# First microseconds of a fused Mamba-2 and feed-forward kernel: idle products, selectors and the first loads

## The chip, the cores and the metric

The kernel runs on one core of a Trainium2 chip. The metric is device microseconds (us) of the whole program. Before the change three runs gave a median of 351.07 us (350.63 to 353.28).

## The reference

Two blocks follow each other. The first is a Mamba-2 state space block for 4 batches, 8 heads, 768 positions, head dimension 32 and state dimension 16. Its recurrence is computed chunk by chunk:

```python
log_a = np.log(np.clip(a, 1e-06, 1.0))
cum = np.cumsum(la, axis=-1)
L = np.exp(cum[:, :, :, None] - cum[:, :, None, :]) * causal
CB = np.einsum('bhin,bhjn->bhij', Cc, Bc)
y = (CB * L) @ xc  +  (Cc @ state) * np.exp(cum)[:, :, :, None]
state = decay_full * state + sum_j Bc x xc * exp(cum[-1] - cum[j])
```

The second takes its output as 3072 tokens of 256 features through a feed-forward block: `h = x @ w_in` (256 to 2048), `g = h * sigmoid(1.702 h)`, `out = g @ w_out` (2048 to 256). The inputs x, a, B and C are float32. The weights are float64 and reach the kernel as pairs of 32-bit words.

## The kernel before

Tokens are worked in six groups of 512, each two "pairs" of two 128-position chunks. For a group the state space part gives `yT` (features on the partitions), then come hidden products with `w_in`, the activation, and products with `w_out`. From the second group on the products are mixed (a scheme with seven products in place of eight). The weights are turned from float64 words to float32 on VectorE and ScalarE piece by piece (`fetch` loads a piece, then `fields`, `clamp`, `rounded`, `join`), and piece i serves a few hidden products, so the first group's hidden products follow the arrival of the weights.

The order on each engine is the order in which the program text issues its instructions; `in_order` at the end fixes it. Waits between engines follow from the data and from the reuse of buffers.

The change touches only the first group, whose start is done in its own way:

- Four loads bring `a` of the first two batches to `az0`, two from SP and two from ScalarE (L274). `load_first` (L134) then loads C with four transfers that ScalarE issues and B with four that SP issues. SP goes on with the first weight piece (`fetch(0)`, L180) and with x of the first two pairs (L150).
- GpSimd makes constants with memsets and affine selects: `pick0` (L300, L303), `ident`, `below` (L316, L318), `same` (L367 to L371, full tile 128x8x32), `pick` (picker, L300 and L303 once more), `whose` (L376, L379), and the zero column of `drop` (L719). `pick` and `whose` are selectors: columns of zeros and ones that pick heads. `part` (VectorE, L387) is summed from `same`.
- `az0` is clamped on VectorE (L338), ScalarE takes the logarithm (L340), and a scan on VectorE makes `cum` (L342).
- On TensorE `keep_busy(5, 0)` (L437) makes five products of ones with ones into the bank `busy`. Nothing reads them. Then eight products with the identity put the causal mask into eight banks (`mask`, L545); `differ` (L551) adds the differences of `cum`, and ScalarE takes the exponential from there (L572). The pool `ps` has four banks, so the bank of the last mask is the one that `busy` had. `pads(n, t)` makes n products of 32 by 32.
- VectorE transposes C and B in 32-blocks (`turn_first`, L612), GpSimd masks C by head (`mask_first`, L645), TensorE turns B back (L624) and makes the scores (L677) and, with `whose`, the rows of `cum` for all heads (L509). VectorE weighs the decays by the scores (`weigh`, L688). Between the two weighings a memset (L171) writes into the buffer of the next weight piece, and SP's next loads (L180, `fetch(1)`) wait for it.
- GpSimd's `since_start` (L662) follows for two pairs. ScalarE's `pick_a` (L363) reads `pick` only in the first group's seventh hidden step.

Of the kernel before, what the change touches and what calls it, by code (L numbers as in the profile page):

```python
# [8 lines left out]
FP32 = mybir.dt.float32  # L9
# [3 lines left out]
ALU = mybir.AluOpType  # L13
AX = mybir.AxisListType

GELU_SCALE = 1.702
P = 128
# [18 lines left out]
def kernel(  # L36
# [31 lines left out]
    nc = tc.nc  # L68
# [4 lines left out]
    NB, NH, S, D = x.shape  # L73
    N = B.shape[-1]
# [10 lines left out]
    PG = CG // 2  # L85
    R = 4
    Q = NH // R
# [7 lines left out]
    const = ctx.enter_context(tc.tile_pool(name="const", bufs=1))  # L95
    raw = ctx.enter_context(tc.tile_pool(name="raw", bufs=3))
    wide = ctx.enter_context(tc.tile_pool(name="wide", bufs=2))
    ssd = ctx.enter_context(tc.tile_pool(name="ssd", bufs=2))
# [30 lines left out]
    def load_first(name, queues):  # L129

        src = {"B": B, "C": C}[name]
        t = blocks[name, 0] = raw.tile([P, 2, PG * P], FP32, tag="z", name=f"z{name}0", bufs=2)
        for r in range(R):
            queues[r].dma_start(  # L134
                out=t[32 * r:32 * r + 32],
                in_=src[0, Q * r:Q * r + Q, :TG].rearrange("q (i f) n -> i q (f n)", i=32))
# [61 lines left out]
    def clamp(i):  # L198


        e = power[i]
        z = e.bitcast(FP32)
        nc.scalar.activation(z, e, AF.Relu, scale=-8.0, bias=edge[:, 0:1])
        nc.scalar.activation(e, z, AF.Relu, scale=-1.0, bias=edge[:, 1:2])
# [68 lines left out]
    for r in range(R):  # L273
        (nc.sync, nc.scalar)[r % 2].dma_start(  # L274
            out=az0[32 * r:32 * r + 32].rearrange("p k s -> p (k s)"),
            in_=a[:2, :, :TG].rearrange("b h (c s) -> (b h) c s", c=PG))
# [3 lines left out]
    def table(f):  # L280

        nc.scalar.activation(early, early, f)

    table(AF.Ln)
    load_first("C", [nc.scalar] * R)
    load_first("B", [nc.sync] * R)
    fetch(0)
    load(0, "x")
# [9 lines left out]
    def picker(name, n, head, group):  # L298
        t = const.tile([P, n, Q], FP32, name=name)
        nc.gpsimd.memset(t, 1.0)  # L300
        for r in range(R):
            rows = t[32 * r:32 * r + 32]
            nc.gpsimd.affine_select(out=rows, in_=rows, pattern=[[-group, n], [-head, Q]],  # L303
                                    compare_op=ALU.is_equal, fill=0.0, base=-head * Q * r,
                                    channel_multiplier=1)
        return t
# [3 lines left out]
    ident = const.tile([P, P], FP32, name="ident")  # L310
# [6 lines left out]
    for side in SIDES:  # L317
        nc.gpsimd.affine_select(out=below[side], in_=below[side], pattern=[[1, H]],  # L318
                                compare_op=ALU.is_ge, fill=-1e5, base=0,
                                channel_multiplier=-1)  # L320
# [9 lines left out]
    def fold_ident(k, engine=nc.vector):  # L330
# [6 lines left out]
    fold_ident(0)  # L337
    nc.vector.tensor_scalar(out=az0, in0=az0, scalar1=1e-6, scalar2=1.0, op0=ALU.max,  # L338
                            op1=ALU.min)
    nc.scalar.activation(cum, az0, AF.Ln)  # L340
    table(AF.Exp)
    nc.vector.tensor_tensor_scan(  # L342
        out=cum.rearrange("p k s -> p (k s)"), data0=carry.rearrange("p k s -> p (k s)"),
# [13 lines left out]
    def pick_a(p):  # L357
# [5 lines left out]
            nc.scalar.activation(X[:, :, q], az[:, c:c + 2], AF.Copy, scale=pick[:, b, q:q + 1])  # L363


    same = ssd.tile([P, NH, D], FP32, tag="BT", name="same")
    nc.gpsimd.memset(same, 1.0)  # L367
    nc.gpsimd.affine_select(
        out=same, in_=same, pattern=[[-N, NH], [0, D]], compare_op=ALU.is_ge,
        fill=0.0, base=0, channel_multiplier=1)  # L370
    nc.gpsimd.affine_select(  # L371
        out=same, in_=same, pattern=[[N, NH], [0, D]], compare_op=ALU.is_ge,
        fill=0.0, base=N - 1, channel_multiplier=-1)
    pick = picker("pick", NB, 1, NH)
    whose = const.tile([32 * PG, 1 + PG, NH, N], FP32, name="whose")
    nc.gpsimd.memset(whose, 1.0)  # L376
    for i, n, head in ((0, 1, PG), (1, 2, PG), (0, 0, 1)):
        t = whose[32 * i:32 * i + 32, n:n + 1]
        nc.gpsimd.affine_select(out=t, in_=t, pattern=[[-1, 1], [-head, NH], [0, N]],  # L379
                                compare_op=ALU.is_equal, fill=0.0, base=-max(n - 1, 0),  # L380
                                channel_multiplier=1)

    part = const.tile([P, Q], FP32, name="part")
    nc.vector.tensor_reduce(  # L387
        out=part, in_=same[:, :, 0].rearrange("p (r q) -> p q r", q=Q), op=ALU.add, axis=AX.X)


    Ls, BE, st = {}, {}, {}
# [33 lines left out]
    def pads(n, t):  # L425

        for i in range(n):
            c = 32 * (i % R)
            nc.tensor.matmul(out=t[c:c + 32, :32], lhsT=ones[:32, :32], rhs=ones[:32, :32],
                             start=True, stop=True, tile_position=(0, c), skip_group_check=True)  # L430

    def keep_busy(n, m):

        t = busy
        pads(m, t)
        for i in range(n):
            nc.tensor.matmul(out=t[:, :3 * H], lhsT=ones,  # L437
                             rhs=ones[:, :H].unsqueeze(1).to_broadcast([P, 3, H]),
                             start=True, stop=True, skip_group_check=True)
# [138 lines left out]
    def bank(name):  # L578
        return ps.tile([P, 4 * P], FP32, tag="ff", name=name)

    def area(name):
        return psa.tile([P, R, 4 * P], FP32, tag="cb", name=name)
# [73 lines left out]
    def since_start(p, engine=nc.vector):  # L656

        b, c = divmod(2 * p, NC)
        s = st[p]
        tp = s["tp"]  # L660
        s["CsT"] = ssd.tile([P, 2, P], FP32, tag="CsT", name=f"CsT{p}", bufs=3)
        engine.tensor_tensor(out=s["CsT"], in0=tp, in1=since[b][:, c:c + 2], op=ALU.mult)  # L662
# [66 lines left out]
    def keep_first():  # L729

        flat_steps = steps.rearrange("p e m -> p (e m)")
        nc.vector.tensor_tensor_scan(
            out=flat_steps, data0=drop.rearrange("p e m -> p (e m)"), data1=flat_steps,
            initial=0.0, op0=ALU.mult, op1=ALU.add)
        for p, copy in zip(range(PG), (nc.vector.tensor_copy, nc.scalar.copy)):
            state[p] = ssd.tile([P, 4, Q * D], FP32, tag="S", name=f"S{p}", bufs=3)
            copy(state[p], steps.rearrange("p e m -> p m e")[:, 4 * p:4 * p + 4])
# [336 lines left out]
    def combine(g):  # L1074


        u, c = copies(g)
        a = acc[g][1]
        scaled(u[:, 2], a[:, 2], u[:, 0])
        scaled(u[:, 1:3], a[:, 3:5], u[:, 2:3].to_broadcast([P, 2, HT]))  # L1080
        scaled(c[:, 1, 0], a[:, 6], u[:, 2])
        scaled(c[:, 0], a[:, 1:6:4], u[:, 0:2])
        plus(c[:, 1, 1], u[:, 2], u[:, 3])
        sums[g] = c
# [51 lines left out]
    def mask_banks(p, r, t, new=True):  # L1136
        ab[p, r] = t[:, :2 * Q * H]
        mask(ab[p, r], new)
# [4 lines left out]
    busy = bank("busy")  # L1143
# [5 lines left out]
                             rhs=ones[:, :H].unsqueeze(1).to_broadcast([P, 4, H]),  # L1149
                             start=True, stop=True, skip_group_check=True)  # L1150

    keep_busy(5, 0)
    both = area("ab0")
    for r in range(R):
        mask_banks(0, r, both[:, r])
    for r in range(R):
        if r == R - 1:
            pads(0, busy)
        mask_banks(1, r, bank(f"ab1_{r}"))
    turn_first("C")  # L1160
    turn_first("B")
# [21 lines left out]
    parts_first()  # L1183
    for p in range(PG):
        since_start(p, nc.gpsimd)
    clamp(0)
    keep_first()
    dense(2)
# [32 lines left out]
    n, p = 2 * PG, 3 * PG  # L1221
# [106 lines left out]
    for g in range(2, NG):  # L1328
        n, p = (g + 1) * PG, (g + 2) * PG
# [14 lines left out]
        def mask_third(k):  # L1344
            if g == 2:
                mask_blocks(k)

        run(g, "1.1 t 0.S P 0.4 P P 1.6 u P 0.3 b 0.T v P 1.5 P 1.7 1.2 P 1.D C", seven(g - 1, 7),
            C=lambda: combine(g - 1), t=turn_third, b=start_third, u=lambda: mask_third(n),
# [82 lines left out]
```

## Time and profile before

| | before |
|---|---|
| median of 3 runs | 351.07 us (350.63 to 353.28) |
| profiled execution: its time | 352.58 us |
| profiled execution: its span, first to last instruction | 350.7 us |
| TensorE busy | 342.9 us, 98% of the span |
| VectorE busy | 255.7 us, 73% |
| ScalarE busy | 149.9 us, 43% |
| GpSimd busy | 13.1 us, 4% |
| DMA | 25.92 MB, mean 74 GB/s |

In the profile PE is TensorE's matmuls and PEld its weight loads, DVE is VectorE, ACT ScalarE, POOL GpSimd, SP the queue that issues most loads; a q behind a name is the engine's sequencer (waits and DMA issues). L with a number is a line of the kernel. One float32 product shows as two records. Starts are in us from the first instruction of the span.

### The profile page before, as it was taken

Reading aid. Unit: us, or ns where it says so; the run is one execution under the profiler, and the core shown is the slowest. Engines: PE = TensorE matmul, PEld = TensorE weight load, DVE = VectorE, ACT = ScalarE, POOL = GpSimd, SP = SyncE. Lnnn points to the kernel's source line nnn. Section 1 sums busy time; section 2 is a strip of 40 time slices with the busy share of each in tenths; the row PEclk is TensorE's granted clock in tenths of the full one; section 3 lists DMA queues with packets and bytes.
Section 4 is the critical chain, followed back from the end, with each engine's and each line's share of the span. In section 5 each row is a group of like instructions: output and inputs, shape, how many; then the busy total and the mean of one; then the engine's idle time right before and its main releaser. Section 6 shows DMA issues by size and latency. Waiting matters only on the chain.

```text
span 350.7 us, 8109 instructions
## 1 busy us (share of the span) xinstructions
PE 342.9 (98%) x3386; PEld 273.8 (78%) x3386; DVE 255.7 (73%) x481; ACT 149.9 (43%) x334; POOL 13.1 (4%) x41
## 2 busy tenths in 40 slices
PE   8889999998999999999999999999999999999996
PEld 7634444546888888888888888888888888889996
DVE  5979999999778999648997457788464654455463
ACT  4788684005353322644432544432554331553320
POOL 8300000100000100000000000000000000000000
PEclk9999999999999999999999999999999999999999
DMA  6599899563625400436604027400000300000301
GB/s 158 110 340 203 223 216 191 85 95 71 111 41 124 72 0 2 75 60 124 115 21 63 0 53 132 76 0 3 0 4 2 54 9 0 0 2 0 62 0 61
DMA packets 89980, 25.92 MB, mean 74 GB/s; under 512 B 73432, under 2 KB 87128, under 8 KB 89944
## 3 DMA queue, kind: packets, MB, share of 16 engines
q1 hardware_dynamic: 89112, 24.88, 34.6%
q10 hardware_dynamic: 832, 0.52, 0.5%
q8 instruction: 26, 0.43, 0.5%
q14 instruction: 10, 0.08, 0.1%
HBM read 22.15 MB, written 3.24 MB: 72 GB/s over the span
## 4 chain that ended last, share of the span: by engine, by line
PE 94%; DVE 2%; DMA 2%; SPq 1%; issue 0%; ACT 0%; DVEq 0%
PE acc L1037 28%; PE X L932 19%; PE Y L942 14%; PE h L876 9%; PE o L974 8%; PE acc L1044 7%; PE y L820 2%; PE cb L677 2%; DMA bits<-in_moe_w_in_dram 2%; PE y L808 1%; PE A L708 1%; PE busy L437 1%; PE ab L551 1%; SPq L180 1%; PE ab L545 0%
## 5 line engine op out<-in xcount | busy, mean ns | idle before, releaser
L937 ACT ACTIVATE ac<-X 128x256 f32<-128x256 f32 x76 | 29.1, 383 | 78.6 <-PE X L932 78.2
L1037 PE MATMUL acc<-mg,mw 128*128 128x256 f32 x192 | 54.5, 379 | 0.0
L909 ACT ACTIVATE gT<-gT 128x512 f32<-128x512 f32 (+1 forms) x76 | 39.3, 520 | 33.9 <-DVE gT L1064 33.3
L1064 DVE TENSOR_TENSOR gT<-Y,ac 128x512 f32<-128x512 f32 x38 | 26.2, 689 | 36.2 <-PE Y L942 30.4
L932 PE MATMUL X<-my,mi 128*128 128x256 f32 x152 | 45.2, 380 | 0.0
L1064 DVE TENSOR_TENSOR gT<-Y,b 128x256 f32<-128x256 f32 x38 | 15.9, 419 | 34.8 <-PE Y L942 34.8
L1037 PEld LDWEIGHTS acc<-mg,mw 128*128 128x128 f32 x192 | 36.5, 190 | 5.0
L876 PE MATMUL h<-yT,w_in 128*128 128x512 f32 (+2 forms) x108 | 35.9, 487 | 1.5 <-DVE w_in L225 1.5
L1037 PE MATMUL acc<-gT,w_out 128*128 128x256 f32 x128 | 35.5, 379 | 0.0
L876 PEld LDWEIGHTS h<-yT,w_in 128*128 128x128 f32 x108 | 18.2, 190 | 17.7 <-issue 15.2
L932 PEld LDWEIGHTS X<-my,mi 128*128 128x128 f32 x152 | 28.0, 190 | 3.9 <-ACT ac L937 0.3
L974 PE MATMUL o<-gT,w_out 128*128 128x512 f32 x64 | 28.6, 597 | 0.0
L900 DVE TENSOR_TENSOR mg<-gT 128x512 f32<-128x512 f32 x40 | 27.2, 681 | 0.0
L1037 PEld LDWEIGHTS acc<-gT,w_out 128*128 128x128 f32 x128 | 24.2, 190 | 3.4 <-ACT yT L847 0.2
L937 ACT ACTIVATE b<-X 128x256 f32<-128x256 f32 x38 | 14.6, 384 | 20.2 <-PE X L932 19.7
L932 PE MATMUL X<-yT,w_in 128*128 128x256 f32 x76 | 23.2, 389 | 0.0
L942 PE MATMUL Y<-my,mi 128*128 128x256 f32 x76 | 22.7, 381 | 0.1
L942 PE MATMUL Y<-yT,w_in 128*128 128x256 f32 x76 | 22.7, 381 | 0.0
L942 PE MATMUL Y<-yT,mi 128*128 128x256 f32 x76 | 22.5, 379 | 0.0
L932 PE MATMUL X<-my,w_in 128*128 128x256 f32 x76 | 22.5, 379 | 0.0
L974 PEld LDWEIGHTS o<-gT,w_out 128*128 128x128 f32 x64 | 11.8, 190 | 13.2 <-issue 12.8
L399 DVE TENSOR_TENSOR_SCAN L<-a,idents 128x1024 f32<-128x1024 f32 x9 | 20.5, 2278 | 0.3 <-DMA a<-scratch 0.3
(152 smaller groups left out, 544.8 us busy)
## 6 DMA issues: line engine op xcount, KB each, us to landing
a<-scratch SPq DMA_DIRECT2D x18, 256.0 KB, 5.3
bits<-in_moe_w_out_dram SPq DMA_DIRECT2D x8, 512.0 KB, 5.1
x<-in_x_dram SPq DMA_DIRECT2D x24, 128.0 KB, 3.6
out_dram<-ob SPq DMA_DIRECT2D x40, 64.0 KB, 1.9
bits<-in_moe_w_in_dram SPq DMA_DIRECT2D x8, 256.0 KB, 5.0
bits<-in_moe_w_in_dram SPq DMA_DIRECT2D x4, 512.0 KB, 8.0
b<-in_B_dram SPq DMA_DIRECT2D x20, 64.0 KB, 2.9
af<-in_a_dram SPq DMA_DIRECT2D x3, 384.0 KB
```

What stands on the lines that cost most here:

```text
L399: nc.vector.tensor_tensor_scan(out=L, data0=ra[p].rearrange("p k e -> p (k e)"), data1=idents.rearrange("p h i -> p (h i)"), initial=0.0, ...
L677: nc.tensor.matmul(out=s["cb"][side, r, k].rearrange("p (q i) -> p q i", q=Q), lhsT=BT[rows, k, side], rhs=CT[rows, k, :, side], start=Tru ...
L876: nc.tensor.matmul(out=h[:, cols], lhsT=w_in[:, f, k], rhs=yT[g][:, k, cols], start=(k == 0 and e == 0), stop=(k == NK - 1), skip_group_ch ...
L900: nc.vector.tensor_tensor(out=t[:, 0:2], in0=B[:, :, 1], in1=B[:, 0], op=ALU.subtract)
L909: nc.scalar.activation(o, i, AF.Silu, scale=GELU_SCALE)
L932: nc.tensor.matmul(out=s["X"], lhsT=lhsT, rhs=rhs, start=i == "1", stop=i == "4", skip_group_check=True)
L937: nc.scalar.activation(copy, s["X"], AF.Copy)
L942: nc.tensor.matmul(out=o, lhsT=lhsT, rhs=rhs, start=s.pop("new", False), stop=i != "5", skip_group_check=True)
L974: nc.tensor.matmul(out=o[c], lhsT=w_out[:, c, f], rhs=gT[g, f // 2][:, f % 2], start=(f == 0), stop=(f == NF - 1), skip_group_check=True)
L1037: nc.tensor.matmul(out=acc[g][0][i][:, cols], lhsT=w, rhs=h[:, cols], start=(j == 0 and k == 0 and (i, 0) in begins), stop=(j == NF // 2 - ...
L1044: nc.tensor.matmul(out=o[k] if type(o) is list else o[:, cols], lhsT=h[:, cols], rhs=w, start=(j == 0 and (i, k) in begins), stop=(j == NF ...
L1064: nc.vector.tensor_tensor(out=o, in0=v, in1=w, op=ALU.add)
```

## The change

`keep_busy` makes three products instead of five, and two 32-by-32 pads go ahead of the last mask. C is loaded with two transfers from each of the two queues, ahead of B on SP's. `same` shrinks to 128x8. `whose` is no longer built by GpSimd: ScalarE copies its three parts from columns of `ident`, ahead of the logarithm. `pick` is built after `since_start`.

```diff
-    load_first("C", [nc.scalar] * R)
+    load_first("C", [nc.sync, nc.scalar] * PG)
     load_first("B", [nc.sync] * R)
     fetch(0)
...
     fold_ident(0)
     nc.vector.tensor_scalar(out=az0, in0=az0, scalar1=1e-6, scalar2=1.0, op0=ALU.max,
                             op1=ALU.min)
+    whose = const.tile([32 * PG, 1 + PG, NH, N], FP32, name="whose")
+    for i, n, head in ((0, 1, PG), (1, 2, PG), (0, 0, 1)):
+        e = 32 * i + max(n - 1, 0)
+        nc.scalar.copy(whose[32 * i:32 * i + 32, n],
+                       ident[32 * i:32 * i + 32, e:e + head * NH:head].unsqueeze(2).to_broadcast(
+                           [32, NH, N]))
     nc.scalar.activation(cum, az0, AF.Ln)
...
-    same = ssd.tile([P, NH, D], FP32, tag="BT", name="same")
+    same = const.tile([P, NH], FP32, name="same")
     nc.gpsimd.memset(same, 1.0)
     nc.gpsimd.affine_select(
-        out=same, in_=same, pattern=[[-N, NH], [0, D]], compare_op=ALU.is_ge,
+        out=same, in_=same, pattern=[[-N, NH]], compare_op=ALU.is_ge,
         fill=0.0, base=0, channel_multiplier=1)
     nc.gpsimd.affine_select(
-        out=same, in_=same, pattern=[[N, NH], [0, D]], compare_op=ALU.is_ge,
+        out=same, in_=same, pattern=[[N, NH]], compare_op=ALU.is_ge,
         fill=0.0, base=N - 1, channel_multiplier=-1)
-    pick = picker("pick", NB, 1, NH)
-    whose = const.tile([32 * PG, 1 + PG, NH, N], FP32, name="whose")
-    nc.gpsimd.memset(whose, 1.0)
-    for i, n, head in ((0, 1, PG), (1, 2, PG), (0, 0, 1)):
-        t = whose[32 * i:32 * i + 32, n:n + 1]
-        nc.gpsimd.affine_select(out=t, in_=t, pattern=[[-1, 1], [-head, NH], [0, N]],
-                                compare_op=ALU.is_equal, fill=0.0, base=-max(n - 1, 0),
-                                channel_multiplier=1)
     part = const.tile([P, Q], FP32, name="part")
     nc.vector.tensor_reduce(
-        out=part, in_=same[:, :, 0].rearrange("p (r q) -> p q r", q=Q), op=ALU.add, axis=AX.X)
+        out=part, in_=same.rearrange("p (r q) -> p q r", q=Q), op=ALU.add, axis=AX.X)
...
-    keep_busy(5, 0)
+    keep_busy(3, 0)
     both = area("ab0")
     for r in range(R):
         mask_banks(0, r, both[:, r])
     for r in range(R):
         if r == R - 1:
-            pads(0, busy)
+            pads(2, busy)
         mask_banks(1, r, bank(f"ab1_{r}"))
...
     for p in range(PG):
         since_start(p, nc.gpsimd)
+    pick = picker("pick", NB, 1, NH)
     clamp(0)
```

## The prediction

> **What bounds the kernel now.** I read the busy table first (TensorE is busy for 98% of the span, so only stretches in which it waits or does filler can be won), then the chain of waits cut to the first 30 us, because every edited line runs there, then the order in time of each engine. The chain, with start, length and owner:
>
> ```profile
> 1.21 3.57 PE busy L437 x10
> 4.78 1.71 PE ab L545 x8
> 6.48 2.60 PE ab L551 x96
> 9.09 0.37 ACT L L572
> ...
> 12.14 1.25 DVE L L688 x2
> ...
> 13.42 0.37 SPq L180
> ...
> 15.63 5.38 DMA bits<-in_moe_w_in_dram
> ...
> 23.33 6.67 PE h L876 x15
> ```
>
> To be seen: the chain begins with five idle products (`keep_busy`, L437) and eight mask products (L545). The decay products (L551) start only when these are through. Then the line is unbroken through exponential (L572), turn back (L624), scores (L677) and the first weighing (L688) to the release of the second weight load (SP, L180), and through that transfer to hidden products 2 and on at 23.33. TensorE idles 1.51 us just before those, so the path through L688 decides, not the first two hidden products. From 23.33 TensorE runs to 37.46 without an idle entry. So a shift of L551 moves the end by as much, if nothing on the way becomes later than it.
>
> The second input of L551 is `cum`, which isn't in this chain. These are rows of all engines in order of time from 4.1 us on (start, length, engine, line; in brackets the idle time before and who ended it):
>
> ```profile
> 4.21 0.45 POOL L371 TENSOR_SCALAR_AFFINE_SELECT same<-same 128x256 f32<-128x256 f32 x1
> 4.22 0.57 DVE L338 TENSOR_SCALAR az<-az 128x256 f32<-128x256 f32 x1 [0.40 <-DMA az<-in_a_dram]
> ...
> 4.83 0.42 ACT L340 ACTIVATE cum<-az 128x256 f32<-128x256 f32 x1 [1.18 <-DVE az L338]
> ...
> 5.28 0.69 DVE L342 TENSOR_TENSOR_SCAN cum<-carry,cum 128x256 f32<-128x256 f32 x1 [0.48 <-ACT cum L340]
> ...
> 7.93 2.03 POOL L645 TENSOR_TENSOR CT<-Ct,part 128x512 f32<-128x512 f32 x2
> ...
> 8.63 1.62 DVE L192 TENSOR_SCALAR p<-bits 128x512 uint32<-128x512 uint32 x1
> ```
>
> `cum` is complete at 5.28 + 0.69 = 5.97; L551's first record begins at 6.41 in the same view, so today TensorE's own queue is 0.44 late. The clamp L338 began 0.01 us after GpSimd's select L371 and ended 0.15 after it; L192, which takes 0.42 to 0.43 us elsewhere, took 1.62 and ended 0.29 after GpSimd's L645 (9.96). Both look blocked by GpSimd.
>
> [...] its record of the granted clock begins at full speed at 6.52 us[...]; the idle products stream 192 columns in 0.32 us, the later filler L1148 256 in 0.22. [...] Here SP spends 0.33 to 0.61 us on each B load.
>
> **The change part by part.**
> - Idle products, five to three. Two products are four records of 0.32: 1.28 us. Masks would begin at 4.57 - 1.28 = 3.29; their operand `below` is complete on GpSimd at 3.21 and identb at 2.75. They run at half clock as now, 0.213 apart: seven end streaming at 4.78.
> - Two pads ahead of the last mask. They write `busy`, whose bank the last mask reuses, so that mask waits for them. No row shows a 32x32 product here; bounds are nothing and 0.5 us (a 128x192 record is 0.53 end to end); I take 0.35. The last mask streams from 5.15 to 5.36. Queued behind it is only L551, which by then waits for `cum`. Cover gone (if `cum` came before 5.36), the cost would be the whole 0.35.
> - GpSimd shorter. `same` falls from three instructions on 128x256 (0.31 + 0.48 + 0.45) to 128x8, about 0.10 + 0.20 + 0.20 by the rows of pick0 (0.10 and 0.19); it ends near 3.9, `drop` near 4.1. So L338 isn't blocked: 4.22 + 0.29 = 4.51, where 0.29 lies halfway by elements between unblocked L192 (512 elements, 0.43) and L322 (4 elements, 0.16). Bounds: nothing gained, if the 0.57 is its own length, to 0.29; I take 0.29, for the two blocked rows agree.
> - Three ScalarE copies ahead of the logarithm. None is in the trace. [...] They wait for `ident` (2.49) and stand behind the table activation (ends 3.65) and ScalarE's second C issue, which now waits for the first load of `a` (landed 3.04) and ends about 3.5. [...] What waits behind them is the logarithm, due at 4.54. [...]
> - `cum`: clamp to 4.51, logarithm 4.54 to 4.96, scan 4.99 to 5.68. L551 begins at 5.74 instead of 6.41: 0.67 earlier.
> - C first on both queues. SP issues two C loads, then four B, the two halves of the first weights and four x: two more than before, about 0.9 us later for all that follows, B's last issue ending near 5.4 instead of 4.44. C's last issue ends at 3.7 instead of 4.19; it landed 2.2 to 2.7 us after its start, so 5.7 to 5.9 instead of 6.49. SP's third B load now waits for the last load of a (landed 4.10), before its own turn at about 4.4: nothing. B: 6.67 becomes 7.4 to 7.6. VectorE: C's transpose 5.95 to 7.0, B's 7.5 to 8.55; TensorE needs B's at 9.45 - 0.6 = 8.85, so 0.3 us spare. First weights: landed 8.53, now 9.0 to 9.4; L192 then no longer meets GpSimd (its two masks end at about 9.1), and L195, Be, L208 end at 11.3 to 11.5, when L688 can start at 12.14 - 0.6 = 11.5: spare 0 to 0.2. x's last load: 11.75 becomes 12.2 to 12.7, which can hold up the gains, but these feed the state and the first hidden products, with the 1.5 us of idle TensorE behind them. SP itself waits 4.3 us for L171 before the next weights.
> - `pick` later: 0.25 + 1.31 us of GpSimd after the two CsT (about 13 us); its first reader is the fan of pair 2, past 35 us. Free; early, it cost GpSimd time only.
>
> Sum: 0.67, less the clock. In the profiled phase L551 would run from 5.74 to 6.52 at half clock: 0.78 us doing 0.39 of work, against 0.05 lost today, so 0.33 is left. [...] I take 0.45. The profiled execution: 350.7 span + 1.9 around it = 352.58, becoming 352.1. It stands 1.5 above the median of the runs; the saving is the same there: 351.07 - 0.45 = 350.6. I hold 350.0 to 351.0 for this case.
>
> **The rivals.**
> - *The clock [...] later (slower).* TensorE has two gaps now, about 0.35 us at the pads and 0.38 before 5.74[...] the turn back and scores take up to 1.3 more: +1.5 to +3, and in the middle 353.3. [...]
> - *The transfers take the place of the wait.* First weights landing after 9.6 or B after 7.9 puts VectorE's row ahead of the scores: the gain is spent and the time is 351.1. For it: the spare of 0.2 us, and a DMA share of 0.77 to 1.20 in every stretch from 4.2 to 9.4 us. Against: with the engines that full, later issue need not be later landing.
> - *The clamp isn't relieved, or the copies are slow.* Then L551 begins at 6.03: 0.38 less the clock's 0.2, 350.9.
>
> **How the numbers follow.** Forecast 0.60, late clock 0.15, transfers 0.15, clamp or copies 0.10. The forecast alone spans 350.0 to 351.0; the runs of before spread over 2.65 us, so a median of three may be off by 0.7, giving 349.3 below. Upwards, the transfers reach 351.8 with that, and the late clock's lower half must be in: 353.0. One per cent, 3.5 us, is about what a measurement of this kernel can tell from no change. Only the far end of the late clock (354.1, with the noise of a median 354.8) gets there: slower 0.05, faster 0.02, same 0.93.
>
> **What would show it.** Right: L338 at 0.3 us; L340 starting by 4.6; L551 by 5.8; L192 at 0.43; L688 near 11.6; hidden product 2 near 22.8. Late clock: the record of full speed begins after 9 us and the L551 rows of 0.65 us are near 1.1. Transfers: an idle entry of L192 or L612 on DMA, and L688 after 12 with TensorE waiting less than VectorE. The forecast is wrong if L688 doesn't move by 0.3 to 0.7, or if it moves and hidden product 2 doesn't.

## The result, and the profile after

The change takes 353.38 us (median; 351.63 to 358.74), the kernel before in the same session 351.71 us (349.62 to 353.71). The ratio is 1.0059, with a 95% interval of 1.0041 to 1.0076: slower by 2.1 us by the ratio and 1.7 by the medians, where 0.45 us less was forecast. Ratios, here and below, leave out executions that took over 1.5% longer than the fastest of their kernel, and the medians keep them. The 351.07 us that the forecast started from is a median of three.

The puzzle is in the profile, which shows nothing of this. Its execution took 351.93 us, near the low end of the change's range, with a span of 350.0 us, and its first microseconds went nearly as the prediction said, step by step. Rows of all engines in order of time (start, length, engine, line, operation; in brackets the idle time before and who ended it):

```profile
3.29 1.70 PE L539 MATMUL ab<-below,identb 128*128 128x256 bf16 x7
...
3.56 0.90 ACT L343 COPY whose<-ident 32x128 f32<-32x128 f32 x3
...
4.21 0.29 DVE L338 TENSOR_SCALAR az<-az 128x256 f32<-128x256 f32 x1 [0.41 <-DMA az<-in_a_dram]
4.53 0.42 ACT L346 ACTIVATE cum<-az 128x256 f32<-128x256 f32 x1
...
4.98 0.69 DVE L348 TENSOR_TENSOR_SCAN cum<-carry,cum 128x256 f32<-128x256 f32 x1 [0.48 <-ACT cum L346]
...
5.73 0.84 PE L545 MATMUL ab<-cum,pick 32*64 32x128 f32 x32
...
11.72 2.36 DVE L682 TENSOR_TENSOR L<-L,cb 128x1024 f32<-128x1024 f32 x2
```

The new copies are L343, which moves the logarithm and the scan to L346 and L348 (before L340 and L342); from `part` (L381) on, line numbers are 6 lower than before. The masks begin at 3.29 instead of 4.57. The clamp takes 0.29 us instead of 0.57, `cum` is complete at 5.67 instead of 5.97, the decay products (L545, before L551) begin at 5.73 instead of 6.41, and the weighing (L682, before L688) at 11.72 instead of 12.14.

The chain of waits of the same execution (start, length, owner) has changed its owner:

```profile
0.80 0.71 SPq L274
...
2.44 0.60 SPq L134
...
6.06 3.62 DMA bits<-in_moe_w_in_dram
...
11.80 1.17 DVE L L682 x2
12.99 0.37 SPq L180
...
15.10 5.26 DMA bits<-in_moe_w_in_dram
20.46 0.43 DVE p L192
```

Before, TensorE's idle products, masks and decay products stood at the head of this chain. Now it runs from SP's issues through the first weights to the weighing and the release of the second weight load at 12.99 (before 13.42). The weighing no longer waits for TensorE's scores but for VectorE's own work on these weights. TensorE follows; these are its hidden products and the fan (`fan_all`, L403, before L409: the first products for the next pair) in order of time:

```profile
22.70 14.15 PE L870 MATMUL h<-yT,w_in 128*128 128x512 f32 x32 [0.74 <-DVE w_in L225]
36.78 0.69 PE L403 MATMUL ab<-X,ones 32*64 32x256 f32 x16
```

Hidden product 2 begins 0.63 us earlier than before (23.33) and the fan 0.68 earlier (37.46). The span is 0.7 shorter. So this one execution looks like the forecast, and the median moved the other way. The cause had to be sought in what one good execution can hide.

### The profile page after: what moved, and what is told of

The parts are those of the page before. It is cut to its first block, busy times and chain, and to the rows that moved or that the text cites. A ratio compares the mean times of both kernels' runs of the same rounds, so it can differ in the third digit from the quotient of the medians.

```text
span 350.0 us, 8109 instructions
## 1 busy us (share of the span) xinstructions
PE 342.8 (98%) x3386; PEld 273.1 (78%) x3386; DVE 254.3 (73%) x481; ACT 150.7 (43%) x337; POOL 11.1 (3%) x37
## 4 chain that ended last, share of the span: by engine, by line
PE 79%; DVE 9%; DMA 6%; SPq 2%; issue 2%; ACT 0%; POOL 0%; DVEq 0%; POOLq 0%
PE acc L1031 28%; PE X L926 19%; PE Y L936 14%; PE acc L1038 7%; PE o L968 4%; DMA af<-in_a_dram 3%; DMA bits<-in_moe_w_in_dram 3%; PE y L814 2%; PE h L870 2%; PE cb L671 2%; DVE p L219 2%; PE y L802 1%; DVE m L208 1%; DVE p L192 1%; DVE m L195 1%
## 5 line engine op out<-in xcount | busy, mean ns | idle before, releaser
L968 PEld LDWEIGHTS o<-gT,w_out 128*128 128x128 f32 x64 | 11.8, 190 | 13.2 <-issue 12.6
```

What stands on the lines that cost most here:

```text
L968: nc.tensor.matmul(out=o[c], lhsT=w_out[:, c, f], rhs=gT[g, f // 2][:, f % 2], start=(f == 0), stop=(f == NF - 1), skip_group_check=True)
```

## Experiments

### Three parts of the change undone, and one alone

First the parts that the prediction had priced: idle products, loads, clock. Idle products and pads as before:

```diff
-    keep_busy(3, 0)
+    keep_busy(5, 0)
...
-            pads(2, busy)
+            pads(0, busy)
```

> The changed kernel with five idle products and no pads again; selectors, GpSimd's setup and the order of the loads stay changed. Late clock (the loss comes from the thinner filler before the decay products): the loss goes, the time is that of before, 351.7 (351.0 to 352.3), 1.7 below the change. Transfers (the loss comes from C ahead of B and later weights and x): it stays at 353.4. The decay products start at 6.4 in both.

Measured: 353.66 us, ratio 1.007 (1.0044 to 1.0095). The loss stays. The reverse, the kernel before with this part of the change alone:

```diff
-    keep_busy(5, 0)
+    keep_busy(3, 0)
...
-            pads(0, busy)
+            pads(2, busy)
```

> The kernel before with only the filler changed: three idle products and two pads. Late clock: the cumulated logarithms come at 5.97 as before, so the gap ahead of the decay products is 0.3 us longer than in the change, and the loss is there in full: 353.4 to 354.4. Transfers: loads are as before, and the decay products start up to 0.4 earlier: 351.3.

Measured: 352.09 us, ratio 1.0008 (0.9988 to 1.0029). The filler isn't the loss. Next, C's loads all on ScalarE again, as before:

```diff
-    load_first("C", [nc.sync, nc.scalar] * PG)
+    load_first("C", [nc.scalar] * R)
```

> The changed kernel with the loads of C and B in the order and on the queues of before. Late clock: the loss stays, 353.0 to 353.5; x lands earlier and can give back 0.3 at most. Transfers: the loss goes and the 0.4 to 0.6 of the earlier decay products shows: 351.2.

Measured: 353.92 us, ratio 1.0086 (1.0056 to 1.0116). And four idle products without pads, so that TensorE has no gap at the pads:

```diff
-    keep_busy(3, 0)
+    keep_busy(4, 0)
...
-            pads(2, busy)
+            pads(0, busy)
```

> The changed kernel with four idle products and no pads, so the masks end streaming at 5.6 and the decay products follow at 5.75 with no gap in between. Late clock: [...] the earlier start is kept: 351.0 to 351.4, below both kernels. Transfers: 353.4.

Measured: 353.81 us, ratio 1.0062 (1.0031 to 1.0092), with a granted clock at full from 4.75 us. Neither the order of the loads nor the clock is the loss. (With C's loads back, the three copies stand behind ScalarE's last issue of C, and L545 begins only at 6.24 in the profile.) What the four slow kernels have in common, and the one that isn't slow lacks, are the selectors and `same`, and there lies something that isn't time: `same` moves from a buffer of the pool `ssd`, which later steps reuse, to a tile of its own in `const`. That is 32 bytes on each partition, and all buffers of `raw`, `wide`, `ssd` and `ffn` are laid out behind it. Before, every one of them began at a multiple of 256 bytes (the first weight buffer `bits` at 79104, which is 309 times 256). In the change every one begins 32 bytes after such a multiple.

### Moving the buffers and nothing else

The kernel before, instruction for instruction, with one small tile made larger:

```diff
-    early = const.tile([P, 1], FP32, name="early")
+    early = const.tile([P, 16], FP32, name="early")[:, :1]
```

> The kernel before, instruction for instruction; one small constant takes 64 bytes a partition instead of 32, so all buffers that are allocated after it, those that the transfers write among them, start 32 bytes further, at odd multiples of 32, as they do in the changed kernel. Place of the buffers (the loss comes from this move): the loss is there without any edit, 353.4 to 353.9. Rival, the remaining edits (the selector copies on ScalarE, GpSimd's shorter setup and later pick): 351.8 as before.

Measured: 353.74 us, ratio 1.0056 (1.0032 to 1.0079). No instruction has changed, and the whole loss is there. With 24 columns in place of 16 the buffers move by 64 bytes:

> As the one before, but the constant takes 96 bytes, so the buffers start 64 bytes further, still at multiples of 64. Place of the buffers by 64: 351.8. If 256 is what counts, 353.4 or more. Remaining edits: 351.8.

Measured: 353.54 us, ratio 1.0053 (1.0033 to 1.0073). The same for the change (`same` as the first columns of a 64-byte tile), and for the change with four products:

```diff
-    same = const.tile([P, NH], FP32, name="same")
+    same = const.tile([P, 2 * NH], FP32, name="same")[:, :NH]
```

> The changed kernel with the shrunken constant same given 64 bytes a partition instead of 32, so that buffers start at multiples of 64 again. Place of the buffers: the loss goes, and what the edits are worth by themselves shows: 351.0 to 351.6. Remaining edits: 353.4.

> The same move by 64 bytes in the changed kernel with four idle products and no pads. Place of the buffers: 350.8 to 351.4, the filler without the gap at the pads. Remaining edits: 353.8.

Measured: 353.58 us, ratio 1.0058 (1.0036 to 1.0079), and 354.3 us, ratio 1.0064 (1.0044 to 1.0083). A multiple of 64 is not enough. Then the kernel before moved by 256 (72 columns) and by 128 (40 columns):

> The kernel before, instruction for instruction; `early` is a column of a 288-byte tile, so that all later buffers lie 256 bytes further and those of the pools raw, wide, ssd and ffn begin at multiples of 256 again. Theory (what counts is whether transfers write from a multiple of 256): as before, 351.4 to 352.0, ratio 1.000 within 0.002, the larger weight loads (512 KB from w_in) landing some 8 us after their issue. Rival (the place itself or any move counts, such as banks or the distance to fixed buffers): 353.5, ratio 1.005.

> The kernel before, instruction for instruction; `early` is a column of a 160-byte tile, so that the buffers of raw, wide, ssd and ffn begin 128 bytes after a multiple of 256. Theory (a multiple of 256 is what counts): the whole loss, 353.2 to 353.8, ratio 1.005. Rival (128 is enough, or only the exact place counts little): 351.4 to 352.0, ratio 1.000 to 1.002.

Measured: 352.00 us, ratio 1.0015 (0.9997 to 1.0033), by 256; 352.92 us, ratio 1.0049 (1.003 to 1.0069), by 128. So of the moves tried, 32, 64 and 128 bytes cost half a per cent and 256 does not: a multiple of 256 is what counts and not the exact place, though a small cost of the place isn't excluded by the first interval.

### Which buffers

Only the four weight buffers `bits` off the multiples of 256 (later on, loads of `a` and mixed weights go to the same buffers), and then the pools `raw`, `ssd` and `ffn` without them; both are the kernel before, instruction for instruction:

```diff
-        return wide.tile([P, 2 * PN], U32, tag="bits", name=name, bufs=BUFS)
+        return wide.tile([P, 2 * PN + 8], U32, tag="bits", name=name, bufs=BUFS)[:, :2 * PN]
...
-        raf[b] = raw.tile([P, NC, P], FP32, tag="af", name=f"af{b}", bufs=1)
+        raf[b] = raw.tile([P, NC * P + 32], FP32, tag="af", name=f"af{b}", bufs=1)[:, :NC * P].rearrange("p (c s) -> p c s", c=NC)
```

> The kernel before, instruction for instruction; only the four buffers `bits`, into which weights (and later `a`) are loaded, leave the multiples of 256: they begin 128, 160, 192 and 224 bytes after one. All other pools' buffers are at multiples of 256. Theory A (writes of the weight loads): the whole loss, 353.3 to 353.8, ratio 1.005, and the 512-KB loads of w_in landing 9 us or more after issue instead of 8.0. Theory B (operands of VectorE, ScalarE or TensorE, or the many small loads of B, C and x): 351.7, ratio 1.000.

```diff
-        power[i] = wide.tile([P, PN], U32, tag="p2", name=f"p2{i}")[:, cols]
+        power[i] = wide.tile([P, PN + 8], U32, tag="p2", name=f"p2{i}")[:, cols]
...
-        raf[b] = raw.tile([P, NC, P], FP32, tag="af", name=f"af{b}", bufs=1)
+        raf[b] = raw.tile([P, NC * P + 56], FP32, tag="af", name=f"af{b}", bufs=1)[:, :NC * P].rearrange("p (c s) -> p c s", c=NC)
...
-    early = const.tile([P, 1], FP32, name="early")
+    early = const.tile([P, 16], FP32, name="early")[:, :1]
```

> The kernel before, instruction for instruction; the reverse: the buffers of raw begin 32 bytes and those of ssd and ffn 64 bytes after a multiple of 256, the weight buffers `bits` and `m` at one (one of the two `p` 32 after). Theory A (writes of the weight loads): 351.7, ratio 1.000. Theory B (compute operands, or the small loads of B, C and x): 353.5, ratio 1.005. In between, about 1.002 to 1.003 in both this and the run before: both kinds of transfer share the loss.

Measured: 352.97 us, ratio 1.0043 (1.0023 to 1.0063), with the weight buffers moved; 352.37 us, ratio 1.0019 (1.0001 to 1.0038), with `raw`, `ssd` and `ffn`. The weight buffers carry most of the loss, by the two ratios, though the intervals overlap; the rest has a share whose interval just leaves out no effect. The two add up to 1.006, about the 1.0056 of all together.

It isn't the engines that read these buffers. Groups by line of VectorE, the kernel before (busy time, mean ns of one, idle before):

```profile
L219 DVE SCALAR_TENSOR_TENSOR p<-bits,p 128x1024 uint32<-128x1024 uint32 x6 | 7.3, 1218 | 0.0
...
L192 DVE TENSOR_SCALAR p<-bits 128x1024 uint32<-128x1024 uint32 x6 | 4.1, 690 | 0.0
```

and the same groups with the weight buffers moved:

```profile
L219 DVE SCALAR_TENSOR_TENSOR p<-bits,p 128x1024 uint32<-128x1024 uint32 x6 | 7.3, 1224 | 0.0
...
L192 DVE TENSOR_SCALAR p<-bits 128x1024 uint32<-128x1024 uint32 x6 | 4.1, 690 | 1.4 <-DMA bits<-in_moe_w_in_dram 0.8 <-DMA bits<-in_moe_w_out_dram 0.6
```

The instructions take the same 690 and 1220 ns, and over the whole span VectorE is busy for 255.7 us in both and ScalarE for 149.7 instead of 149.9; what is new is 1.4 us of waiting for the loads. In the stretch of the weight loads the DMA engines take longer for a byte. One row of the table by stretches (14 to 60 us; at its end the granted clock, the DMA share and GB/s), first the kernel before:

```profile
14.00:60.00 46.00, 43.69 (x300) 20.84 (x293) 42.38 (x61) 33.92 (x53) 0.74 (x1) 1.00 0.94 233
```

then the same moved by 32 bytes:

```profile
14.00:60.00 46.00, 43.68 (x301) 20.88 (x300) 39.24 (x58) 31.00 (x50) 0.74 (x1) 1.00 0.97 229
```

More busy time for fewer bytes. Summed over the records of the packets that start in that stretch, a megabyte costs each of the 16 DMA engines 43.45 us / 10.70 MB = 4.06 us before and 44.66 / 10.56 = 4.23 us moved by 32. Over the eight profiles with all buffers at multiples of 256 (two of them from the last part of the experiments) it is 3.85 to 4.06, mean 3.97; over the nine with all moved it is 4.06 to 4.23, mean 4.14; with the weight buffers alone moved 4.14, with `raw`, `ssd` and `ffn` alone 3.98. The ranges touch: with the instructions of the kernel before it is 4.02 (moved by 256) and 4.06 against 4.06, 4.14 and 4.23 (moved by 128, 64 and 32). The means differ by 4%, on some 10.5 MB an estimated 1.8 us more work for the DMA engines in a stretch in which their share is 0.85 to 0.97. The 1-KB packets of the first weights (16 to 30 us) take 52.4 to 55.3 ns unmoved and 55.2 to 56.9 moved. How long the 512-KB loads take to land, which two expectations named as a sign, is none: medians of 8.0 to 10.9 us in the eight unmoved profiles and of 9.1 to 12.1 in the nine moved.

Where this reaches TensorE shows at a hidden product near 34 us. In the profile with the weight buffers moved, in order of time:

```profile
34.90 3.67 PE L876 MATMUL h<-yT,w_in 128*128 128x512 f32 x8 [1.50 <-DVE w_in L225]
```

TensorE waits for VectorE's converted weights (L225); VectorE itself had waited 0.35 and 0.49 us for their pieces (L192, at 26.79 and 31.07). Seven of the nine profiles with all moved have this wait at over 0.5 us (0.67 to 1.88); the change's own and that with five products don't. Of the eight unmoved, three have it (1.17, 1.05 and 0.70), and the one with `raw`, `ssd` and `ffn` moved has none. So it comes more often off the multiples of 256, but it isn't confined to them.

A longer wait follows in some executions. The waits of the kernel before moved by 32 (this execution took 356.09 us, its kernel's median is 353.74; engine, line, releaser: us in total, times, longest):

```profile
PE A L708 <- DVE CsT L662: 2.6, 1, 2.6
PE h L876 <- DVE w_in L225: 1.6, 2, 0.9
...
DVE p L192 <- DMA bits<-in_moe_w_out_dram: 3.3, 1, 3.3
```

and in its stretches, with the granted clock third from the end:

```profile
66.00:69.00 3.00, 0.38 (x11) 0.19 (x14) 2.32 (x4) 0.00 (x0) 0.93 (x3) 0.95 0.61 74
69.00:72.00 3.00, 3.00 (x119) 2.50 (x119) 2.97 (x3) 0.00 (x0) 0.13 (x1) 0.50 0.64 111
```

In before's profile TensorE had no wait between 23.33 and 81 us. Here VectorE waits 3.3 us for a piece of `w_out` (L192), so what is queued behind it on VectorE is late too, TensorE stands still for 2.62 us up to 68.95, and from 68.69 to 72.10 its clock is halved. That last step isn't in every execution: a mean granted clock of 0.995 or less was seen in 25 of 165 executions with all buffers moved, in 2 of 110 of five variants with none moved (filler alone, both moved by 256, and the two in the old place below), and in none of 22 with the weight buffers alone moved. With the kernel before moved by 128, such executions took 355.25 us on average, the others 353.00, so most of the loss is there without it. That the longer transfers make up the whole loss by way of these waits is argued from sizes that fit (1.8 us of work, waits of 0.67 to 2.62 us); the runs show that the place of the buffers costs it.

### The change without the move

Now the change with its buffers at multiples of 256: first `same` as a slice of a 256-byte tile, then `same` back in its old buffer, so that every address of the four pools is that of before.

```diff
-    same = const.tile([P, NH], FP32, name="same")
+    same = const.tile([P, 64], FP32, name="same")[:, :NH]
```

> The change, with `same` the first 8 columns of a 256-byte tile, so that the pools' buffers begin at multiples of 256 again. Theory: the first microseconds give what they gave in the profile of the change, without the later loss: 350.9 to 351.5, ratio 0.997 to 0.999, TensorE without idle time before the hidden products near 34 us and the scores near 67 us. Rival (the change itself holds a loss that the moved buffers only look like): 353.5, ratio 1.005.

```diff
-    same = const.tile([P, NH], FP32, name="same")
+    same = ssd.tile([P, NH * D], FP32, tag="BT", name="same")[:, :NH]
```

> The change, with `same` taken from the first 8 columns of its old buffer in ssd, so that raw, wide, ssd and ffn lie exactly where they lay before. Theory 1 (the predicted 0.45 to 0.67 us of the first microseconds reach the end): 350.7 to 351.1, ratio 0.998. Theory 2 (the weight loads, late by themselves in some executions, take the place of the start as what TensorE waits for): 351.4 to 351.9, ratio 1.000 to 1.001.

Measured: 351.94 us, ratio 1.0011 (0.9991 to 1.0031), and 351.97 us, ratio 1.0009 (0.9992 to 1.0027). Against 1.0059 the loss is gone to four fifths or more. But the forecast gain, 0.9987, isn't there; both intervals just leave it out, and the expectation of the first run (0.997 to 0.999) was missed. The profile of the second shows a possible reason. TensorE in order of time:

```profile
4.92 0.32 PE L423 MATMUL busy<-ones 32*32 32x32 f32 x4
5.30 0.37 PE L539 MATMUL ab<-below,identb 128*128 128x256 bf16 x1
5.72 1.16 PE L545 MATMUL ab<-cum,pick 32*64 32x128 f32 x32
...
10.76 1.12 PE L618 MATMUL b<-ident,Bt 128*128 128x128 f32 x4 [0.46 <-ACT L L566]
...
14.05 1.16 PE L671 MATMUL cb<-CT,Bt 32*64 32x128 f32 x32
```

L545 begins early, at 5.72, but its 32 records take 1.16 us (0.69 at full clock), and so do the scores (L671) at 14.05: the record of the full clock begins only at 17.43. With C's loads back on ScalarE, four idle products and no pads in that kernel:

```diff
-    keep_busy(3, 0)
+    keep_busy(4, 0)
...
-            pads(2, busy)
+            pads(0, busy)
...
-    load_first("C", [nc.sync, nc.scalar] * PG)
+    load_first("C", [nc.scalar] * R)
```

> As the run before, with keep_busy(4, 0), no pads and C's four loads on ScalarE as in the kernel before: what is left of the change is GpSimd's shorter setup, ScalarE's copies and one idle product fewer, so that the first weights land as early as before. Theory 1: 350.6 to 351.1. Theory 2 with the first weights as the cause: 351.0, and the run before stays at 351.6. Theory 2 with the later weights: as the run before.

Measured: 351.82 us, ratio 0.9995 (0.9977 to 1.0012), full clock from 4.77 us. This misses the first expectation (350.6 to 351.1) and fits the last, that the later weights take the place of the start. One of its 22 executions is above 353 us, against 7 of 22 in the run before it and 9 of 59 of the kernel before beside them. It is the best version of the change by its median, and not to be told from the kernel before; its interval holds the forecast 0.9987 too. But the early start isn't in it: in its profile ScalarE's copies run from 4.23 to 5.14, behind its last issue of C, and L545 begins at 6.24 instead of 6.41.

### The start itself: a later one, and less filler

Two idle products more in the kernel before (`keep_busy(7, 0)`), and one only, without pads, in the change with `same` in its old place (`keep_busy(1, 0)`):

> The kernel before with keep_busy(7, 0): two idle products more, masks and decay products 1.28 us later, nothing else. If the start is the bound: +1.0 to +1.3 us, 352.6 to 352.9, ratio 1.003 to 1.004. If the weight loads pace the first hidden products and the start has slack: ratio 1.000 to 1.001, and hidden product 2 within 0.4 us of where it was.

> The change with `same` in its old place, keep_busy(1, 0) and no pads. If little idle work opens the clock late: full speed from 9 us or later in the profile, the decay products' rows of 32 near 1.16 us instead of 0.69 to 0.84, and +0.5 to +2 us against the same with three products, ratio 1.002 to 1.006. If the filler doesn't matter: full speed by 7.5 us and ratio 1.000 to 1.001.

Measured: 352.23 us, ratio 1.0022 (1.0005 to 1.0039), with seven; 355.15 us, ratio 1.0112 (1.0081 to 1.0143), with one. The first falls between its two expectations, and its profile tells part of why; TensorE in order of time:

```profile
5.74 1.04 PE L545 MATMUL ab<-below,identb 128*128 128x256 bf16 x8
6.71 0.69 PE L551 MATMUL ab<-cum,pick 32*64 32x128 f32 x32
...
24.08 14.26 PE L876 MATMUL h<-yT,w_in 128*128 128x512 f32 x32 [2.05 <-DVE w_in L225]
38.28 0.69 PE L409 MATMUL ab<-X,ones 32*64 32x256 f32 x16
```

In this execution the record of the full clock begins at 5.63, before the masks, which took 1.04 us (1.91 in the profile of before, where it begins at 6.52): L551 is 0.30 us later than before, not 1.28. Hidden product 2 and the fan are 0.75 and 0.82 later, more than the start can account for: 0.28 lies ahead of the release of the second weight load (13.70 instead of 13.42), the rest in that load and the work on it. The whole kernel is 0.2% slower, with an interval that just leaves out no effect. How much of it is the later start, these runs don't separate. The kernel with one product shows the other side:

```profile
1.21 1.00 PE L431 MATMUL busy<-ones 128*128 128x192 f32 x2 [1.21 <-DVE ones L296]
3.23 1.87 PE L539 MATMUL ab<-below,identb 128*128 128x256 bf16 x8 [1.02 <-POOL below L318]
5.80 1.16 PE L545 MATMUL ab<-cum,pick 32*64 32x128 f32 x32 [0.70 <-DVE part L381]
```

In this execution, with gaps of 1.02 and 0.70 us, the clock is full only from 17.82 us. The time is 355.15 - 351.97 = 3.2 us above that with three products and pads, more than the 0.5 to 2 expected.

## Why the prediction was wrong

**The step that failed** is "GpSimd shorter. `same` falls from three instructions on 128x256 ... to 128x8". It was priced in GpSimd's time alone. The same edit moves `same` from `ssd` to `const`, so it gives every buffer behind it a new address, and the sum has no term for that. The missing term is the change as it stands against the change with its buffers at multiples of 256: 1.0059 - 1.0011 = 0.0048, or 1.7 us of 351.4. Where the kernel before is moved, it is 0.0049 to 0.0056, or 1.7 to 2.0 us. What remains, 0.1% with an interval that holds no effect, is all that the priced parts did.

A second step failed beside it: the gain of the start, 0.45 us, isn't in the medians even with the buffers back at multiples of 256. The 0.45 was the author's estimate, between 0.67 and the 0.33 that is left if the clock rises at 6.52 as in the profile of before; in the profile of the change it rises at 6.10.

**The steps priced at the start were right in the profile up to the weighing, and nearly all by their size.** Masks at 3.29 (as said); pads 0.32 (0.35 taken); clamp 0.29 (0.29); `cum` at 5.67 (5.68); L545 at 5.73 (5.74); weighing at 11.72 (11.5 to 11.6). Two could have cost more than they did in that execution. The three copies, whose length no trace of before shows, took 0.90 (281 to 298 ns each, at a pitch of 0.30, so they don't overlap); ending at 4.46, they stayed inside ScalarE's idle time ahead of the logarithm, which began at 4.53. And the first weights landed at 9.68 instead of 9.0 to 9.4, with L192 at 0.43 us as forecast: GpSimd's two masks had ended at 9.00.

**That hidden product 2 came at 22.70 (22.8 forecast) is luck in good part.** The kernel before moved by 128 has the same instructions as the kernel before. All engines in order of time:

```profile
6.01 0.69 PE L551 MATMUL ab<-cum,pick 32*64 32x128 f32 x32
...
11.73 2.36 DVE L688 TENSOR_TENSOR L<-L,cb 128x1024 f32<-128x1024 f32 x2
...
21.62 10.54 PE L876 MATMUL h<-yT,w_in 128*128 128x512 f32 x24 [0.43 <-DVE w_in L225]
```

Here the clock rose at 5.53 and not at 6.52, and the weighing begins where the change has it. Over the seven profiles with the instructions of the kernel before, the weighing begins at 11.73 to 12.54 and hidden product 2 at 21.62 to 23.50. The change's 22.70 lies inside that, so one profile against one could not show a gain of 0.6 us behind the second weight load.

**"So a shift of L551 moves the end by as much"** is the second step. It does not hold in the profile of the change moved by 256:

```profile
33.73 3.67 PE L870 MATMUL h<-yT,w_in 128*128 128x512 f32 x8 [1.05 <-DVE w_in L225]
37.33 0.69 PE L403 MATMUL ab<-X,ones 32*64 32x256 f32 x16
```

There the weighing begins at 11.37 and the second weight load is released at 12.64, 0.77 and 0.78 us before the profile of before, and the fan comes 0.13 before it: TensorE waits 1.05 us for weights at 33.73, and 0.80 at 66.61, waits that the profile of before didn't show. "TensorE runs to 37.46 without an idle entry" was read from one execution, and the transfers leave little behind it. How large a share of the missing gain this is stays open.

**The rival of the late clock** names something that occurs, a late rise, but it isn't the loss: with five products the change is as slow (1.007 against 1.0059). When the clock would rise in the change, and the 1.5 to 3 us that a late rise would cost, were the author's estimates: the trace of before shows one rise, at 6.52. Of six profiles with three products and pads (the change, filler alone, loads back, moved by 64, by 256, and in the old place), two rise late, at 10.68 and 17.43 us; of twelve with four products or more, all rise from 4.75 to 7.42. What decides it isn't shown: in the profiles of the change and of the change in the old place TensorE's first products start within 0.01 us of each other up to L545 (1.21, 3.29, 4.92, 5.31 and 5.73 against 1.21, 3.29, 4.92, 5.30 and 5.72), and the clock rises at 6.10 in the one and at 17.43 in the other. Late executions may have eaten part of the forecast gain: the late rise at 17.43 puts the weighing at 15.31. But this is argued. A profile shows the clock's rise of one execution only, and executions above 353 us are not clearly more frequent with three products in place (7 of 22 in the old place and 6 of 22 moved by 256, against 9 of 59 and 11 of 75 of the kernel before).

**The rival of the transfers** named the right resource and, for the loss, the wrong stretch. It feared later issue of the first loads. Their landing at 9.68 did pass its point of decision (9.6), and VectorE's row became what the weighing waits for, but the gain wasn't spent there: the weighing still began 0.42 us earlier. The loss is tied to the addresses of the buffers that the later weights go to. Undoing the order of the loads brought nothing (1.0086 against 1.0059, intervals overlapping).

**The chances.** 0.5% of loss lies inside "within 1%", which had 0.93, but for a reason that no rival had, and outside the range, whose upper end of 353.0 came from the late clock.

## To carry to other kernels

A tile that changes its pool or size shifts every buffer behind it: list the addresses before and after, and where transfers set the pace, as with the weights here, try their destinations at multiples of 256 bytes (32 to 128 bytes off them cost the kernel before 0.5%). To test for it, make one unused column wider, which changes no instruction. And a profile is one execution: where the profile is better and the median worse, look for a cost that comes and goes, such as waits for transfers, and look at several profiles of one program before a gain of half a microsecond is read from two.

## What was not expected of the hardware

- Destinations of loads that begin 32, 64 or 128 bytes after a multiple of 256 make this kernel 0.5% slower (1.0049 to 1.0056 with not one instruction changed), at 4.14 us of DMA engine time for a megabyte on average against 3.97. The losses at 32 and at 128 bytes are alike (1.0056 and 1.0049). What in the transfer costs the time is not shown here.
- Packets of 128 bytes show the move by themselves: mean 12.5 ns where the pool `raw` begins at a multiple of 128 or 256, 13.0 to 13.2 ns where it begins 32 or 64 after one, in every profile.
- The record of the full clock can begin as late as 17.43 us, with the rows of 32 records at 1.16 us until then and not at 0.69, although TensorE has no gap above 0.46 us from its first product until then (the change with `same` in its old place; TensorE is busy for 10.35 of the 10.8 us from 6.6 to 17.4). Over the profiles of before, the change and the runs it begins at 4.75 to 7.42 us, at 10.68, at 17.43 and, with one idle product, at 17.82.
